# One linear step of an exponential moved from VectorE to GpSimd, with a ring buffer and two more exp tiles

## The chip, the cores and the metric

The kernel runs on one core of a Trainium2 chip. The metric is the device time of one execution in microseconds (us), the median of several runs. In some of them the record shows a TensorE clock below full speed for some time: a mean of 0.986 instead of 0.998 goes with about 10 us more in the kernel before (942 us instead of 932).

Engines are named as the profile names them: PE is TensorE (PEld its weight loads), ACT is ScalarE, DVE is VectorE, POOL is GpSimd.

## The reference, cut to what matters

The program is one conformer block on x of shape (2, 4000, 144), four heads of 36, in bfloat16. Only the attention concerns us:

```python
h = _layernorm(x, axis=-1)
qkv = h @ w_qkv
# ... split into q, k, v, four heads each ...
scores = jnp.einsum('bhqd,bhkd->bhqk', q, k) * scale
p = _softmax(scores, axis=-1)
att = jnp.einsum('bhqk,bhkd->bhqd', p, v)
```

A feed-forward layer stands before it; a convolution module, a second feed-forward layer and a last normalisation stand behind it.

## The kernel before

The kernel is a Python program that draws up its own schedule. `Rec.op` records an instruction, gives it a start by a small cost model (when its engine is free, when its inputs are ready), and keeps that order. A list scheduler picks what to record next; its choices hang on tables of numbers (`POLICY`), one value for each of 49 stretches of the run. When all is recorded, each engine gets its instructions in the recorded order, with semaphore waits between engines. An engine whose next instruction is late stands still; e8_sel50 below shows such a stop of 4.18 us.

Queries are worked in 16 chunks of 500; each chunk has 63 score tiles (62 full ones of 128 x 1000, a small one at the end). PE makes the scores in PSUM. The exponential is then made in one of two ways. ACT does it in one instruction. For 137 of the tiles DVE does it in a chain: it writes the exponent as an integer (two casts out of PSUM), splits the fraction off (AND), forms a parabola of it (linear step, square), adds that back and halves. The halved 16-bit integer is the bit pattern of a bfloat16.

```python
op("dve", "tensor_scalar", mm, zz, 0xFF, 0x6400, op0=ALU.bitwise_and, op1=ALU.bitwise_or, ...)   # AND
yield need("dve")
off, sc = (E2[1] - 1) / (2 * E2[2]), (256 * E2[2]) ** 0.5
op("dve", "tensor_scalar", mf, mf, sc / 256, (off - 4) * sc, op0=ALU.mult, op1=ALU.add, ...)     # linear step
yield need("dve")
op("dve", "tensor_tensor", mf, mf, mf, op=ALU.mult, ...)                                         # square
yield need("dve")
op("dve", "tensor_tensor", zz, zz, mf, op=ALU.add, ...)                                          # add
# ... give back tile y ...
op("dve", "tensor_scalar", zz, zz, 256 * (E2[0] - 1) - (off * sc) ** 2, 0.5, op0=ALU.add, op1=ALU.mult, ...)  # halve
```

`zz` and `mm`/`mf` are two views into exp tiles (`PT`, nine of them). PE then multiplies the tile with the values. GpSimd normalises rows for the layers around the attention (`XN<-X,RS` in the profile).

The softmax here doesn't subtract the row's maximum and nothing guards it: scores larger than these inputs give would overflow.

## Time and profile before

| | before |
|---|---|
| time, median (lowest to highest) | 932.76 us (931.62 to 932.99, 3 runs) |
| ACT, DVE, POOL busy | 895.0, 849.9, 306.1 us of 929.6 |
| exp tiles of 1000 columns on ACT / on DVE | 855 / 137 |

The lines of the profile that carry the reading stand in the prediction below. The chain of waits that ended last, by engine:

```profile
ACT 47%; PE 36%; DVE 14%; issue 1%; POOL 1%; DMA 0%; POOLq 0%; DVEq 0%
```

ACT and PE hand work to each other for 83% of the span.

### The profile page before, as it was taken

The numbers are of one execution on the slowest core, as the hardware profiler recorded it, in microseconds if no ns is written. First come the engines' busy times: TensorE is split into PE (matmuls) and PEld (weight loads), VectorE is DVE, ScalarE is ACT, GpSimd is POOL, SyncE is SP. The second block draws the span as 40 slices with busy tenths as digits, with TensorE's granted clock in tenths as the row PEclk, the third lists the DMA queues.
The fourth block names the chain that finished last, engine by engine and source line by source line (L and its number), as shares of the span: only waits on it lengthen the run. The fifth ranks groups of instructions, "written<-read, shape, count | busy, mean of one in ns | idle before, by whom it ended". The sixth has DMA issues, their size and how long they took to land.

```text
span 929.6 us, 26576 instructions
## 1 busy us (share of the span) xinstructions
PE 886.9 (95%) x11413; PEld 405.4 (44%) x11413; DVE 849.9 (91%) x1880; ACT 895.0 (96%) x1142; POOL 306.1 (33%) x520
## 2 busy tenths in 40 slices
PE   8999999999999999999999999999999999999997
PEld 7444433434344344344443443443444343434456
DVE  8886799999989999998999999898999999997997
ACT  6899999999999999999999999999999999999985
POOL 4220140182115412351512452225415331441433
PEclk9999999999999999999999999999999999999999
DMA  4000000000000000000000000000000000000000
GB/s 124 22 2 1 2 2 1 1 2 1 2 2 2 2 2 2 2 2 1 9 1 1 14 2 8 2 1 14 2 8 3 7 2 9 8 1 8 8 2 26
DMA packets 7449, 7.30 MB, mean 8 GB/s; under 512 B 2381, under 2 KB 7332, under 8 KB 7332
## 3 DMA queue, kind: packets, MB, share of 16 engines
q1 hardware_dynamic: 5918, 5.00, 1.8%
q8 instruction: 89, 1.46, 0.6%
q10 hardware_dynamic: 1414, 0.62, 0.3%
q14 instruction: 28, 0.23, 0.1%
HBM read 3.31 MB, written 2.30 MB: 6 GB/s over the span
## 4 chain that ended last, share of the span: by engine, by line
ACT 47%; PE 36%; DVE 14%; issue 1%; POOL 1%; DMA 0%; POOLq 0%; DVEq 0%
ACT PT L169 41%; PE PS L169 36%; DVE PT L169 8%; ACT TH L169 5%; DVE ST L169 2%; DVE HT L169 1%; DVE X L169 1%; DVE QT L169 1%; DVE OTF L169 1%; POOL RS L169 0%; DMA X<-in_x_dram 0%; DVE DG L169 0%; POOL XN L169 0%; DVE XN L169 0%; DVE XT L169 0%
## 5 line engine op out<-in xcount | busy, mean ns | idle before, releaser
L169 ACT ACTIVATE PT<-PS 128x1000 bf16<-128x1000 f32 (+1 forms) x871 | 802.4, 1053 | 6.8 <-PE PS L169 5.2
L169 PE MATMUL PS<-QT,KT 64*64 64x500 bf16 x3968 | 413.9, 385 | 20.3 <-ACT PT L169 14.2
L169 PE MATMUL PS<-PT,VA 64*37 64x500 bf16 x3968 | 353.4, 374 | 4.9 <-DVE OTF L169 2.2
L169 PEld LDWEIGHTS PS<-QT,KT 64*64 64x64 bf16 x3968 | 122.4, 104 | 219.7 <-ACT PT L169 139.1
L169 POOL TENSOR_SCALAR RS<-ST 125x4 f32<-125x4 f32 x112 | 41.6, 371 | 467.2 <-DVE ST L169 462.5
L169 DVE TENSOR_SCALAR PT<-PS 128x500 uint16<-128x500 f32 x274 | 183.0, 669 | 12.8 <-PE PS L169 11.5
L169 DVE TENSOR_TENSOR PT<-PT 128x1000 uint16<-128x1000 uint16 (+1 forms) x274 | 184.0, 676 | 1.5
L169 DVE TENSOR_SCALAR PT<-PT 128x1000 uint16<-128x1000 uint16 (+1 forms) x411 | 163.8, 415 | 2.3
L169 PEld LDWEIGHTS PS<-PT,VA 64*37 64x37 bf16 x3968 | 114.1, 95 | 111.1 <-issue 31.9
L169 POOL TENSOR_SCALAR XN<-X,RS 125x144 bf16<-125x144 bf16 x224 | 149.9, 680 | 5.8
L169 POOL TENSOR_TENSOR RS<-RS,NHALF 125x4 f32<-125x4 f32 (+1 forms) x103 | 100.5, 980 | 112.5 <-DVE RS L169 107.8
L169 ACT ACTIVATE TH<-PS 128x500 bf16<-128x500 f32 (+2 forms) x198 | 104.3, 549 | 5.0 <-PE PS L169 4.3
L169 DVE SCALAR_TENSOR_TENSOR HT<-TH,PS 128x500 bf16<-128x500 bf16 (+1 forms) x135 | 80.8, 614 | 9.6 <-ACT TH L169 9.4
L169 PE MATMUL PS<-XT,WA 72*128 72x500 bf16 (+2 forms) x288 | 73.8, 355 | 2.9 <-DVE HT L169 1.6
L169 DVE SCALAR_TENSOR_TENSOR X<-PS,X 125x288 bf16<-125x288 f32 x128 | 57.0, 451 | 15.3 <-PE PS L169 13.6
L169 DVE BATCH_NORM_STATS2 ST<-X 125x6 f32<-125x288 bf16 x160 | 65.5, 446 | 1.2 <-DMA X<-in_x_dram 1.0
L169 PE MATMUL PS<-WB,HT 128*125 128x144 bf16 (+1 forms) x640 | 52.8, 230 | 0.5 <-DVE HT L169 0.5
L169 PEld LDWEIGHTS PS<-WB,HT 128*125 128x125 bf16 (+1 forms) x640 | 44.1, 136 | 14.0 <-issue 4.2
L169 PE MATMUL PS<-IDENT,XN 125*72 125x125 bf16 x512 | 42.2, 221 | 2.5 <-DVE HT L169 1.3
L169 DVE COPY XT<-PS 72x1000 bf16<-72x1000 bf16 (+1 forms) x66 | 39.9, 609 | 3.1 <-PE PS L169 2.6
L169 PEld LDWEIGHTS PS<-IDENT,XN 125*72 125x72 bf16 x512 | 31.5, 112 | 21.0 <-issue 10.6
L169 PE MATMUL PS<-U,DG 128*128 128x250 bf16 (+5 forms) x204 | 34.3, 265 | 0.6 <-DVE PT L169 0.4
(88 smaller groups left out, 579.6 us busy)
## 6 DMA issues: line engine op xcount, KB each, us to landing
X<-in_x_dram SPq DMA_DIRECT2D x16, 140.6 KB
out_dram<-XN SPq DMA_DIRECT2D x13, 140.6 KB
out_dram<-XN SPq DMA_DIRECT2D x4, 70.3 KB
WA<-in_w_ff1a_dram ACTq DMA_DIRECT2D x1, 144.0 KB
WB<-in_w_ff1b_dram ACTq DMA_DIRECT2D x1, 144.0 KB, 2.6
WA<-in_w_ff2a_dram SPq DMA_DIRECT2D x1, 144.0 KB
WB<-in_w_ff2b_dram SPq DMA_DIRECT2D x1, 144.0 KB
WQKV<-in_w_qkv_dram ACTq DMA_DIRECT2D x1, 121.5 KB
```

The lines of the kernel that those rows point to most:

```text
L169: ins = getattr(eng, o.name)(*o.a, **o.k)
```

## The change

The intent: DVE is nearly full while GpSimd is idle two thirds of the time. If GpSimd does the linear step, DVE has room for more tiles, and ACT, the fullest engine, has fewer to do. The trip over GpSimd keeps exp tiles longer, so two are added; their memory comes from `XTQ`, which held the normed rows of a whole batch (4000 columns) and becomes a ring of four chunks. All schedule tables are new.

```diff
-    NPT = 9
+    NPT = 11
+    XR, XD = 4, 16
     ... (every POLICY table has new values) ...
+    GPOOL = 1
+    GSLACK = 1.5
+    GCOST = 1.6
-    XTQ = sb("XTQ", [2, T])
+    XTQ = sb("XTQ", [2, XD + XR * CH])
     ... (projections read XTQ at c % XR; the last 16 columns are copied for tiles across the seam) ...
     def pre2(c):
-        yield need("dve")
+        yield need("dve", cond=lambda: c < XR or (c - XR in q_done and c - XR + 1 in v_done))
     ...
-        yield need("dve")
+        pool = GPOOL and R.free["pool"] < R.free["dve"] + GSLACK
+        yield need("pool" if pool else "dve")
-        op("dve", "tensor_scalar", mf, mf, sc / 256, (off - 4) * sc, op0=ALU.mult, op1=ALU.add, r=[("M", y, 0)],
-           w=[("M", y, 1)], cost=c_dve(2 * CH, 4))
+        op("pool" if pool else "dve", "tensor_scalar", mf, mf, sc / 256, (off - 4) * sc, op0=ALU.mult, op1=ALU.add,
+           r=[("M", y, 0)], w=[("M", y, 1)], cost=GCOST if pool else c_dve(2 * CH, 4))
```

## The prediction

> **What bounds the kernel now.** I read the busy table first, then the windows by stage, then the groups of instructions, then short stretches of the timeline. The page's first table (engine, busy us, share of the span, instructions):
>
> ```profile
> PE 886.9 (95%) x11413; PEld 405.4 (44%) x11413; DVE 849.9 (91%) x1880; ACT 895.0 (96%) x1142; POOL 306.1 (33%) x520
> ```
>
> Three engines stand over 90%, so the table alone does not name the bound. The Trainium skill, "Perfetto Trace Analysis", section "Identifying the Most-Contended Engine", says to judge VectorE, ScalarE and GpSimd by occupancy, and that matmul occupancy is a poor measure of how close TensorE is to its limit; weight-load occupancy is better. Here weight loads are 44%, so I set PE's 95% aside and look at the others by stage (columns: window, length, then PE, PEld, DVE, ACT, POOL busy us with counts, clock, DMA share, GB/s):
>
> ```profile
> 0.00:50.00 50.00, 45.31 (x540) 30.03 (x541) 42.41 (x137) 36.63 (x63) 17.53 (x37) 1.00 0.24 68
> 50.00:150.00 100.00, 97.02 (x1254) 40.20 (x1254) 78.89 (x195) 97.75 (x121) 19.41 (x33) 1.00 0.01 2
> 150.00:200.00 50.00, 47.88 (x646) 21.19 (x642) 48.69 (x102) 49.47 (x60) 17.71 (x28) 1.00 0.01 2
> 200.00:900.00 700.00, 673.81 (x8697) 293.86 (x8694) 657.25 (x1367) 693.92 (x861) 240.82 (x407) 1.00 0.02 4
> 900.00:930.00 30.00, 22.89 (x291) 20.13 (x288) 22.63 (x82) 17.22 (x41) 10.60 (x15) 0.97 0.07 21
> ```
>
> From 200 to 900 us ACT is busy 693.92 of 700 (99%) and DVE 657.25 (94%). ACT is the bound of the long middle, with DVE close behind; GpSimd stands at 34% there. Only the first 50 and the last 30 us leave ACT idle (13 us each), and the change does not address those. The groups that matter (name, count | busy, mean ns | idle before):
>
> ```profile
> L169 ACT ACTIVATE PT<-PS 128x1000 bf16<-128x1000 f32 x855 | 794.4, 1061 | 5.6 <-PE PS L169 4.0
> L169 DVE TENSOR_SCALAR PT<-PS 128x500 uint16<-128x500 f32 x274 | 183.0, 669 | 12.8 <-PE PS L169 11.5
> L169 DVE TENSOR_SCALAR PT<-PT 128x1000 uint16<-128x1000 uint16 x274 | 110.0, 415 | 1.5
> L169 DVE TENSOR_TENSOR PT<-PT 128x1000 uint16<-128x1000 uint16 x137 | 92.4, 677 | 0.6
> L169 DVE TENSOR_TENSOR PT<-PT 128x1000 f16<-128x1000 f16 x137 | 92.3, 676 | 0.9
> L169 DVE TENSOR_SCALAR PT<-PT 128x1000 f16<-128x1000 f16 x137 | 56.9, 415 | 0.8
> L169 POOL TENSOR_SCALAR XN<-X,RS 125x144 bf16<-125x144 bf16 x224 | 149.9, 680 | 5.8
> ```
>
> The softmax's exponential is made in two ways: 855 full tiles by one ScalarE instruction, 137 tiles by a seven-instruction VectorE chain. The split is the balance between the two engines: each tile that VectorE takes over is one less on ACT. The change frees VectorE, so it pays only as far as more tiles go over (or VectorE's lateness was holding ACT, which the 1% idle in the middle says it hardly was).
>
> Recorded lengths overlap by the write's tail, so I take starts. ACT: seven exp tiles in a row occupy 699.77 to 705.95, 0.88 us each. DVE: start to start, an AND 0.33, a PSUM cast 0.59, the linear step 0.32; two tensor-by-tensor steps took 1.38 together at 405.59, the next at 406.89, 0.65 each.
>
> ```profile
> 699.77 6.42 ACT L169 ACTIVATE PT<-PS 128x1000 bf16<-128x1000 f32 x7
> 705.95 0.51 ACT L169 ACTIVATE TH<-PS 128x250 bf16<-128x250 f32 x1
> ...
> 226.07 0.41 DVE L169 TENSOR_SCALAR PT<-PT 128x1000 uint16<-128x1000 uint16 x1
> 226.40 0.67 DVE L169 CAST QT<-PS 128x500 bf16<-128x500 f32 x1
> 226.99 0.41 DVE L169 TENSOR_SCALAR PT<-PT 128x1000 f16<-128x1000 f16 x1
> 227.31 0.67 DVE L169 CAST QT<-PS 128x500 bf16<-128x500 f32 x1
> ```
>
> So a VectorE tile costs that engine 2 x 0.59 + 2 x 0.65 + 3 x 0.33 = 3.5 us now, and 3.1 us without the linear step.
>
> **What the Trainium skill says.** "SBUF — State Buffer", section "SBUF: two separate sides": VectorE and GpSimd share one pair of SBUF ports as an exclusive lock; a VectorE instruction in a two-port mode, or with two SBUF inputs, and a GpSimd instruction block each other, whichever starts first. Four of the chain's steps are of that kind: the AND, the two tensor-by-tensor steps, the last add. The trace agrees with blocking, but not evenly. Durations, min/median/max:
>
> ```profile
> L169 POOL TENSOR_SCALAR XN<-X,RS x224: 453/462/3222, 127.4 to 895.4; 125x144 bf16<-125x144 bf16 x112
> L169 DVE TENSOR_SCALAR PT<-PT x411: 365/409/603, 91.8 to 894.3; 128x1000 uint16<-128x1000 uint16 x97, 128x1000 f16<-128x1000 f16 x40
> L169 DVE TENSOR_TENSOR PT<-PT x274: 626/668/825, 94.0 to 893.3; 128x1000 f16<-128x1000 f16 x124, 128x1000 uint16<-128x1000 uint16 x13
> ```
>
> A GpSimd row can be pushed from 0.46 to 3.22 us; a VectorE step loses at most 0.2 us. Laying the starts side by side, VectorE is delayed when it starts some 180 to 310 ns after a GpSimd row's start, and then until about 315 ns after it: a 144-element row holds the ports some 150 ns, about 1.05 ns an element, though its record lasts 460. A GpSimd row thus yields to VectorE before it has begun and blocks it while it streams. At 1000 elements the hold would be some 1.05 us, seven times longer, and no VectorE step in this trace has met that. "GPSIMD Engine Reference", section "Elementwise — side-by-side cycle accounting", gives 1.03 cycles an element for simple bodies; the 1.05 ns is near it.
>
> **The change, part by part.**
> (a) Removed from VectorE: up to one 0.33 us step per tile, 137 x 0.33 = 45 us at most. The builder moves it only if it thinks GpSimd free within 1.5 us of VectorE. GpSimd's normalisation bursts (two small steps, a power of about 1.04 us, four rows) occupy a third of the middle, so I choose 85%: 116 steps, 38 us.
> (b) Added to GpSimd: some 0.2 fixed + 1.05 streaming = 1.25 us alone (estimate from the rows above), about 1.6 with the waits that rows show here (mean 680 against 462). 116 x 1.6 = 186 us, so GpSimd goes to about 490 us, 53%. Not a bound, but rows and steps queue behind one another.
> (c) Port stalls put back on VectorE. I put a hold of 1.05 us at each of the 137 linear steps of this trace, let it wait for a VectorE step under way, and counted the following port-using steps, except the square that needs its result: 41 are hit, 15 us in all, 0.11 us each. With a 1.4 us hold it is 0.25 us. I take 0.11 x 116 = 13 us.
> (d) Net VectorE time freed: 38 - 13 = 25 us. Spending x more tiles there costs 3.1x and shortens the run by 0.88x, which at 91% use takes 0.8x of VectorE's room: 25 = 3.9x, x = 6 to 7, **6 us off ACT's path**.
> (e) Buffers: nine to eleven exp tiles. A VectorE tile holds two through its chain, and the GpSimd hop lengthens it by over 1 us; the two extra tiles mostly pay for that.
> (f) The ring for normed rows: projections of chunk c wait for chunk c-4's queries and values. In the first batch this pulls queries of chunks 2 and 3 forward, three to five casts of 0.59 us each into a stretch where VectorE has room (79% from 50 to 150 us). About zero. A copy of 16 columns every fourth chunk is nothing.
> (g) The retuned schedule tables: nothing in the profile prices them. ACT's idle in the middle is 6 us, so they can win 2 or 3 us there and as much at the ends. I allow 3 us.
> Sum: 932.8 - 6 - 3 = about **924 us**.
>
> **The rivals.** *The port lock gives it all back*: if the step holds the ports 1.4 us or more, stalls reach 0.25 us and over, and the square waits for a late GpSimd. Then VectorE frees nothing, the planned extra tiles make it late, ACT starves: 930 to 938. For it: a 3.22 us row; the builder's cost model has no lock. Against: VectorE lost at most 0.2 us so far. *All gain, no stall*: 45 us freed, x = 45/3.9 = 11.5, 10 us off, with retuning about 918; against it stands the lock. *GpSimd becomes a bound*: normalised rows come late and projections starve; at 53% I do not believe it. *A transfer matters*: DMA share is 0.02; no.
>
> **Range and chances.** Between full gain with good retuning (915) and everything given back (933). Over 2% faster needs under 914.5, which is beyond the no-stall sum; 0.10. Over 2% slower needs over 951; 0.03.
>
> **What will show it.** A group of GpSimd steps writing exp tiles, about 116, mean near 1.6 us; more than 137 PSUM-read pairs on VectorE (about 144) and fewer than 855 ACT tiles (about 848); the maxima of AND and tensor-by-tensor steps rising from 603 and 825 ns to 1.4 us or more; ACT still 99% busy in the middle. I am wrong if VectorE takes over 12 tiles or more, if the tile count is unchanged but the time falls (then buffers or retuning did it), or if the square's wait for GpSimd shows among the longest waits.

## The result, and the profile after

| | before | after |
|---|---|---|
| time, median (lowest to highest) | 932.88 us (931.62 to 933.14, 4 runs) | 944.66 us (944.53 to 944.97, 4 runs) |
| ratio, 95% interval | | 1.0129 (1.0112 to 1.0147) |
| exp tiles of 1000 columns on ACT / on DVE | 855 / 137 | 850 / 142 |

The changed kernel is 1.3% slower, outside the range of the prediction.

The changed kernel's busy table, and two of its windows (same columns as in the prediction):

```profile
PE 889.9 (94%) x11420; PEld 402.5 (43%) x11420; DVE 851.0 (90%) x1802; ACT 895.2 (95%) x1138; POOL 436.8 (46%) x633
```

```profile
200.00:900.00 700.00, 665.18 (x8550) 286.58 (x8547) 653.00 (x1291) 681.13 (x841) 356.63 (x506) 1.00 0.02 4
900.00:945.00 45.00, 34.44 (x418) 25.06 (x416) 31.99 (x95) 29.13 (x56) 14.82 (x24) 0.95 0.05 14
```

ACT's busy total is the same as before to 0.3 us. Between 200 and 900 us it is busy 681.13 us where it was busy 693.92: 12.8 us more idle. The loss builds up there: the work missed in the middle is done after 900. (Busy time is not a pure measure of work: e1_pow below has the same ACT instructions and reads 890.0 us busy, 5.2 less. Five tiles fewer on ACT, some 4.4 us by the prediction's 0.88 us each, therefore don't show in this total.) DVE is no fuller than before, so the bound did not move to it. The chain of the changed kernel:

```profile
PE 34%; DVE 30%; ACT 30%; POOL 4%; issue 1%; DMA 0%; POOLq 0%; DVEq 0%
```

DVE's share of the chain went from 14% to 30%. Its groups in the changed kernel (count | busy, mean ns | idle before), to be set against the same groups in the prediction:

```profile
L169 DVE TENSOR_SCALAR PT<-PT 128x1000 uint16<-128x1000 uint16 x284 | 125.2, 453 | 1.2
L169 DVE TENSOR_TENSOR PT<-PT 128x1000 uint16<-128x1000 uint16 x142 | 103.0, 728 | 0.6
L169 DVE TENSOR_TENSOR PT<-PT 128x1000 f16<-128x1000 f16 x142 | 97.6, 689 | 2.2 <-POOL PT L169 2.1
```

The AND and halving steps grew from 415 to 453 ns, the adds from 677 to 728, the squares from 676 to 689. The square's wait for GpSimd is only 2.1 us in the whole run, so the trip as such is hidden. The durations as min/median/max tell how the means grew:

```profile
L169 DVE TENSOR_SCALAR PT<-PT x319: 364/411/1128, 101.4 to 906.2; 128x1000 uint16<-128x1000 uint16 x140, 128x1000 f16<-128x1000 f16 x20
L169 DVE TENSOR_TENSOR PT<-PT x284: 627/669/1498, 104.2 to 905.3; 128x1000 f16<-128x1000 f16 x126, 128x1000 uint16<-128x1000 uint16 x16
```

The medians stayed, the maxima nearly doubled: a minority of steps is held up. The moved step on GpSimd:

```profile
L169 POOL TENSOR_SCALAR PT<-PT x107: 1024/1029/2310, 101.9 to 901.6; 128x1000 f16<-128x1000 f16 x107
```

One such hit in the changed kernel's timeline, DVE first (start us, length us), then GpSimd:

```profile
815.12 0.45 DVE L169 TENSOR_TENSOR AN<-PS,RD 125x288 bf16<-125x288 f32 x1
815.49 1.35 DVE L169 TENSOR_TENSOR PT<-PT 128x1000 uint16<-128x1000 uint16 x1
816.76 0.41 DVE L169 TENSOR_SCALAR PT<-PT 128x1000 uint16<-128x1000 uint16 x1
```

```profile
815.29 1.02 POOL L169 TENSOR_SCALAR PT<-PT 128x1000 f16<-128x1000 f16 x1 [1.25 <-DVE PT L169]
```

The add starts 0.20 us after the GpSimd step and takes 1.35 us instead of 0.67: if its usual length is taken off the end, it stands still until 0.88 us after that step's start, and only then runs. Laid side by side, the hits on a GpSimd step that was not itself delayed all end their standstill 0.88 to 0.89 us after its start. A DVE step that is already under way goes first, and the GpSimd step is the longer one. One that begins just after the GpSimd step is mostly shut out: of the three chain steps that began in its first 0.17 us, those at 0.11 and 0.15 us were held up by 0.77 and 0.83 us, and only the third went first. So the step shuts DVE out until 0.88 us after its start. (The expectations below, and the planner of e11_aware, reckon with a hold of 0.72 us that begins 0.165 us after the start. These traces don't bear out that free beginning.)

How that reaches ACT shows on PE (the group of the matmuls with the values, before and after; idle before, what ended it):

```profile
L169 PE MATMUL PS<-PT,VA 64*37 64x500 bf16 x3968 | 353.4, 374 | 4.9 <-DVE OTF L169 2.2 <-ACT PT L169 1.0 <-DVE PT L169 0.8
L169 PE MATMUL PS<-PT,VA 64*37 64x500 bf16 x3968 | 357.5, 375 | 9.3 <-DVE PT L169 6.1
```

Before, these matmuls waited 0.8 us for DVE's tiles; now 6.1. In PE's recorded order the next scores stand behind them, so they come late and ACT waits for them. ACT's waits for PE ahead of exponentials, before and after (us in total, times, longest):

```profile
ACT PT L169 <- PE PS L169: 5.2, 16, 0.5
ACT PT L169 <- PE PS L169: 14.6, 32, 1.3
```

### The profile page after: what moved, and what is told of

It reads as the page before. It is cut to its first block, busy times and chain, and to the rows that moved or that the text cites. A ratio compares the mean times of both kernels' runs of the same rounds, so it can differ in the third digit from the quotient of the medians.

```text
span 942.8 us, 26578 instructions
## 1 busy us (share of the span) xinstructions
PE 889.9 (94%) x11420; PEld 402.5 (43%) x11420; DVE 851.0 (90%) x1802; ACT 895.2 (95%) x1138; POOL 436.8 (46%) x633
## 4 chain that ended last, share of the span: by engine, by line
PE 34%; DVE 30%; ACT 30%; POOL 4%; issue 1%; DMA 0%; POOLq 0%; DVEq 0%
PE PS L169 34%; ACT PT L169 26%; DVE PT L169 19%; ACT TH L169 4%; DVE ST L169 2%; DVE HT L169 2%; POOL RS L169 2%; DVE X L169 2%; POOL XN L169 2%; DVE XT L169 1%; DVE QT L169 1%; DVE SW L169 1%; DVE AN L169 0%; DMA X<-in_x_dram 0%; DVE U L169 0%
## 5 line engine op out<-in xcount | busy, mean ns | idle before, releaser
L169 PE MATMUL PS<-PT,VA 64*37 64x500 bf16 x3968 | 357.5, 375 | 9.3 <-DVE PT L169 6.1
L169 POOL TENSOR_SCALAR PT<-PT 128x1000 f16<-128x1000 f16 x107 | 123.2, 1151 | 302.6 <-DVE PT L169 301.6
L169 DVE TENSOR_SCALAR PT<-PS 128x500 uint16<-128x500 f32 x284 | 189.3, 669 | 18.5 <-PE PS L169 17.2
L169 DVE TENSOR_TENSOR PT<-PT 128x1000 f16<-128x1000 f16 (+1 forms) x284 | 199.4, 709 | 2.9 <-POOL PT L169 2.1
L169 DVE TENSOR_SCALAR PT<-PT 128x1000 uint16<-128x1000 uint16 (+1 forms) x319 | 139.3, 450 | 1.4
L169 POOL TENSOR_TENSOR RS<-RS,NHALF 125x4 f32<-125x4 f32 (+2 forms) x101 | 97.0, 965 | 81.4 <-DVE RS L169 76.6
L169 DVE SCALAR_TENSOR_TENSOR HT<-TH,PS 128x500 bf16<-128x500 bf16 (+1 forms) x140 | 83.4, 614 | 14.9 <-ACT TH L169 14.5
L169 POOL TENSOR_SCALAR RS<-ST 125x4 f32<-125x4 f32 x114 | 43.9, 385 | 95.4 <-DVE ST L169 89.4
L169 DVE SCALAR_TENSOR_TENSOR X<-PS,X 125x288 bf16<-125x288 f32 (+1 forms) x128 | 57.1, 451 | 10.4 <-PE PS L169 9.0
```

The costliest lines, as they stand in the source:

```text
L169: ins = getattr(eng, o.name)(*o.a, **o.k)
```

## The experiments

**Theory.** The GpSimd step shuts the ports that the DVE chain needs. The order of all engines was drawn up by a cost model that knows no ports. A stall that the order does not know of makes DVE late, then PE, then ACT, and the bound engine's lost time is not won back. **Rivals.** The trip over GpSimd itself (hop); the new tables being worse on the chip; the step simply belonging on DVE.

Building one part of the change without another is no clean test: any edit that alters a recorded cost or choice shifts every later choice. So most experiments keep the recorded order of all engines **exactly** and replace the instruction that is issued at a place. The replay then is:

```diff
-                    ins = getattr(eng, o.name)(*o.a, **o.k)
+                    todo = getattr(o, "pre", []) + [(o.name, o.a, o.k)] + getattr(o, "post", [])
+                    for name, args, kw in todo:
+                        ins = getattr(eng, name)(*args, **kw)
```

**e1_pow: same trip, ports free.** A power of 125 x 4 numbers takes GpSimd as long as the step (mean 1146 against 1151 ns) but reads and writes next to nothing. The result lacks the correction.

```diff
+        if pool:
+            o.name, o.a, o.k = "tensor_tensor", (SCR[0:TB, y, 0, :], PONE[0:TB, :], NHALF[0:TB, :]), dict(op=ALU.pow)
-        op("dve", "tensor_tensor", mf, mf, mf, op=ALU.mult, ...)
+        op("dve", "tensor_tensor", mf, mf, mf, op=ALU.subtract if pool else ALU.mult, ...)
     ... (the halving step gets another constant)
```

> The changed kernel with the order of every engine's instructions untouched; only the 107 linear steps on GpSimd are replaced by a power of 125x4 numbers (1.04 us, the same length as the step's 1.02 to 1.03 us alone) that waits for the AND and is waited for by the square in the same way, but hardly touches SBUF. Wrong on purpose (the square becomes a difference, so the correction is left out). PORT THEORY (the step holds the SBUF ports some 0.72 us, VectorE stalls by about 20 us in sum, and the fixed order turns that into about 16 us of lateness): the time falls by 12 to 16 us, to 929 to 933. HOP RIVAL (the trip over GpSimd, not the ports, makes the square and all behind it late): within 3 us of 944.7. TABLES RIVAL (the new schedule tables are just worse on the chip): within 3 us of 944.7.

Measured: 930.91 us (930.69 to 931.05), 13.8 us less than the changed kernel; the kernel before took 931.71 in the same rounds (ratio 0.999). The DVE groups and the middle window of e1_pow:

```profile
L171 DVE TENSOR_SCALAR PT<-PT 128x1000 uint16<-128x1000 uint16 x284 | 114.4, 415 | 1.2
L171 DVE TENSOR_TENSOR PT<-PT 128x1000 uint16<-128x1000 uint16 x142 | 95.9, 678 | 0.6
L171 DVE TENSOR_TENSOR PT<-PT 128x1000 f16<-128x1000 f16 x142 | 95.6, 675 | 2.1 <-POOL SCR L171 1.9
```

```profile
200.00:900.00 700.00, 672.95 (x8690) 293.58 (x8689) 646.50 (x1317) 686.99 (x856) 361.08 (x514) 1.00 0.02 4
```

The lengths are back at 415, 678 and 675 ns. Against these the changed kernel's stalls sum to 284 x 38 + 142 x 50 + 142 x 14 ns = 19.9 us. Taking them away, with order and trip unchanged, takes 13.8 us off the time, and DVE's share of the chain falls from 30% to 12%: the port theory holds, hop and tables fall as the cause of the loss. One us of stall cost 0.69 us. The run says a second thing: **without any stall from the step, the change is worth 0.8 us at most** (the interval of the ratio, 0.9973 to 1.0007, includes no gain), though DVE was relieved of 107 steps of 0.33 us, 35 us in all. The tiles did come off ACT: over the whole run it is busy 890.0 us against 895.0 in the kernel before. But its idle time grew from 34.6 to 39.3 us, and its waits for PE ahead of the tile `TH` alone from 4.3 to 9.6 us.

**e2_split2, e4_hold2, e5_pow2: the size of hold and trip.** The step as two halves; the step after a second pass into a scratch tile; two powers.

```diff
 # e2_split2: o becomes the first half, the second follows at once
+            parts_ = [(o.name, (mf[:, j:j + 500], mf[:, j:j + 500]) + tuple(o.a[2:]), o.k) for j in range(0, 2 * CH, 500)]
 # e4_hold2
+            o.pre = [(o.name, (SCH[:, nsc[0] % 4, :],) + tuple(o.a[1:]), o.k)]
 # e5_pow2: as e1_pow, and once more
+            o.post = [(o.name, (SCR[0:TB, y, 1, :],) + o.a[1:], o.k)] * 1
```

> Same order; each linear step on GpSimd is two instructions of 500 elements, so each holds the ports half as long. Right results. PORT THEORY: stalls about half as long for about as many hits, 5 to 8 us less, 937 to 940. HOP RIVAL: the step takes about 0.2 us longer in all, so no gain, 945 to 950. TABLES RIVAL: 943 to 947.

> Same order; each GpSimd step is preceded by a second pass of the same size into a scratch tile, so ports are held twice as often and the trip takes about 2 us (the plan reckons with 1.6). Right results. PORT THEORY: stalls about double, plus some waits of the square: 15 to 30 us more, 960 to 975. TABLES RIVAL: under 955.

> As e1_pow, but with two powers one after the other: the trip takes about 2 us as in e4_hold2, the ports stay free. Wrong on purpose. PORT THEORY: within 6 us of e1_pow (929 to 939), far below e4_hold2. HOP RIVAL: close to e4_hold2, 955 or more.

Measured: 943.54, 984.78 and 949.97 us. Only e4's direction came as foretold, and it went past its range; the other two missed. (e2 lies in the range of the tables rival, which e1_pow had already ruled out.) The two doubled trips both make the square wait for GpSimd (waits of DVE in e4_hold2, then in e5_pow2: us in total, times, longest):

```profile
DVE PT L171 <- POOL PT L171: 29.4, 40, 1.5
```

```profile
DVE PT L171 <- POOL SCR L171: 28.0, 45, 1.9
```

At 1.15 us the trip makes the squares wait only 1.9 us in all (e1_pow); with two powers it costs 19 us more. The order had been drawn up with 1.6 us. At nearly equal trips e4 is 34.8 us over e5, and 32.3 us if only runs at full clock are taken (981.6 against 949.3). By the same sum its stalls come to 37.9 us, about twice the changed kernel's: twice the stall cost more than twice e1's 13.8. The split halved the stalls (284 x 22 + 142 x 24 + 142 x 7 ns = 10.6 us) but brought 1.1 us. Two things may have eaten the rest, and no run parts them: the squares' waits for GpSimd rose from 2.1 to 7.1 us, and TensorE's clock was lowered in all four runs of e2 (0.985 to 0.996; the changed kernel had 0.998 to 0.999). In the profiled one it was at half for 6.8 us after a pause of PE of 1.64 us. Whether smaller holds are a remedy stays open.

**e3_ondve: the same order, the steps on DVE.**

```diff
+        if pool:
+            o.lin = True                     # at emission
+            if getattr(o, "lin", False):     # when all is recorded, ahead of the semaphores
+                o.eng = "dve"
```

> The changed kernel, order untouched, with the 107 linear steps put back on VectorE at the places where GpSimd was to do them: VectorE gets 107 x 0.33 = 35 us that the order has no room for, the ports are free of the step. LATENESS THEORY (in a fixed order each us of unplanned VectorE time costs about 0.68 us: e1_pow took 20.2 us of stall away and gained 13.8 us): 930.9 + 0.68 x 35 = 955, 948 to 960. RIVAL (the step belongs on VectorE, the move to GpSimd is the fault by itself): faster than 944.7, near e1_pow, 930 to 940.

Measured: 948.85 us, at the low end: 35 us that the order did not know of cost 17.9 us over e1_pow, 0.5 per us (the trip is gone in e3 as well). The rival falls; the moved step costs more on DVE than on GpSimd in *this* order.

**e7_inject: unplanned DVE time in the kernel before.** Is it ports at all, or any time that the order does not know of?

```diff
+        if n % 2 == 0:
+            o.pre = [(o.name, (SCH[:, :], zz[:, 0:CH]) + tuple(o.a[2:]), o.k)]    # a second AND, 500 elements
```

> The kernel before with its order untouched; 65 of its 137 VectorE tiles get one extra AND of 500 elements into a scratch tile in front of their own AND, about 0.20 us each, 13 us in all that the order does not know of; no GpSimd step, no new port use by GpSimd. LATENESS THEORY at 0.68 a us: 9 us more, 937 to 944. RIVAL (VectorE stood 6% idle in the middle, such time is absorbed): under 935.

Measured: 941.88 us against 932.08. The 65 extra steps take 13.1 us from start to next start and cost 9.8 us, 0.75 per us, in a kernel whose DVE stood 6% idle in the middle. (Two of the four runs had a slightly lowered clock; the two at full clock took 941.3 us, 0.7 per us.) No step was moved to GpSimd, and the chain's lengths stayed (418, 674 and 676 ns). An extra AND is of the kind that shares ports, so a small part may be GpSimd's lateness: its rows took 705 ns in the mean instead of 680. In the main the price is that of lateness in a fixed order; in the changed kernel the ports are what made DVE late.

**e6_nopool: the new tables without the step.**

```diff
-    GPOOL = 1
+    GPOOL = 0
```

> The changed kernel built with the GpSimd step switched off; ring, eleven exp tiles and new tables stay, so the builder draws up another order. TABLES RIVAL (the tables are good, the step spoils them): 925 to 932. THEORY (tables are fitted to one order each and are worth nothing once it shifts): 938 to 950, no better than the changed kernel although no step holds the ports.

Measured: 952.14 us, above even the range given. Nothing holds the ports, and it is slower than both. The edit makes the builder draw up another order, for which the tables were never fitted; it can't tell what the step is worth, and I read no more from it.

**e8_sel50, e9_sel75, e10_sel49: the step moved only where the ports are free.** In the order of the kernel before, with its tables and nine tiles, a linear step goes to GpSimd only if the order has room for the trip, no port-using DVE step begins meanwhile and GpSimd is idle.

```diff
+    for o1, o2, o3, o4 in chain:                 # AND, linear step, square, add
+        t0 = o1.t0
+        if o3.t0 - t0 < 1.45:                    # e9: 1.1
+            continue
+        if any(t0 + 0.45 < p < t0 + 1.35 and p not in (o1.t0, o2.t0, o3.t0) for p in ports):
+            continue
+        if any(p0 < t0 + 1.45 and p1 > t0 + 0.3 for p0, p1 in busy):     # e9: 1.1
+            continue
+        if before_[id(o2)] > t0 + 0.4:           # e10 only
+            continue
     ... (the step's time is added to busy)
+        o2.eng = "pool"
```

> The kernel before with its order untouched (nine exp tiles, old tables, no ring); only those 50 of 137 linear steps go to GpSimd for which the plan shows at least 1.45 us from the AND to the square, no port-using VectorE step starting in between, and GpSimd idle. Right results. LATENESS THEORY: next to no stall is added (under 3 us in sum against 20 in the changed kernel), 50 x 0.33 = 16 us of VectorE time is freed, which can win back part of the 7 us by which the old order runs behind its plan: 926 to 930. RIVAL (any port-holding step on GpSimd costs more than it frees): 933 to 938. RIVAL (freed VectorE time is worth nothing in a fixed order): 931 to 933.

> As e8_sel50 with the shorter limit of 1.10 us from AND to square: 75 steps move, some of which make the square wait for GpSimd by up to 0.5 us. LATENESS THEORY: little more than e8 or a loss, 927 to 933. If trips did not matter: 1 to 2 us below e8.

Measured: 938.74 and 963.28 us, both misses, though the stalls are as small as before. In e8 most of it is one event. GpSimd, then DVE and PE in e8's timeline:

```profile
575.26 1.80 POOL L171 TENSOR_SCALAR XN<-X,RS 125x144 bf16<-125x144 bf16 x4
...
577.15 1.03 POOL L171 TENSOR_SCALAR PT<-PT 128x1000 f16<-128x1000 f16 x1
578.22 0.68 DVE L171 TENSOR_TENSOR PT<-PT 128x1000 f16<-128x1000 f16 x1 [4.18 <-POOL PT L171]
...
579.54 0.60 PE L171 MATMUL PS<-XT,WA 72*128 72x500 bf16 x2 [3.48 <-DVE HT L171]
```

My selection looked at planned times, but GpSimd runs in recorded order, and this step had been recorded behind a normalisation that comes later. DVE waited 4.18 us, PE stood still 3.48 us. The next window shows a second price (TensorE's granted clock is third from the right):

```profile
580.00:582.50 2.50, 2.50 (x19) 0.71 (x22) 2.47 (x7) 1.63 (x3) 0.00 (x0) 0.58 0.00 0
```

The clock fell to half for 3.4 us after PE's pause. The Trainium skill, "TensorE: Matmul & The Clock Gate", section "What's actually happening", says that after an idle window of about 3.4 us the array's clock drops to half; this trace agrees. (Other profiles here show the half clock after shorter pauses; see the last section.) e9 has several such events (mean clock 0.979 to 0.984 in all its runs). Without that step:

> As e8_sel50 without the one step that e8's trace shows stuck on GpSimd behind a later normalisation row (VectorE waited 4.2 us for it at once). If that queue place was e8's whole loss: 931 to 934. If freed VectorE time did win something once it is gone: 926 to 930. If the other 49 trips cost something too: 935 or more.

Measured: 933.18 us against 931.70 (ratio 1.0017, interval 1.0001 to 1.0034). So the queue place and what followed it was most of e8's loss, and moving 49 steps at next to no stall, 16 us of DVE time freed, wins nothing. In a fixed order no tile can go over from ACT, so this run doesn't test what freed time is worth to an order drawn up for it.

**e11_aware, e13_aware_pow: a builder that knows of the ports.** The cost model gets the port rule with the numbers that I had read from the traces (the start of the hold set too late, see above), and the tables were searched again for its own order.

```diff
-    GCOST = 1.6
+    GCOST = 1.03
+    HOLD = 0.72
     # in Rec.op
+        if hold:
+            h0 = start + 0.165
+            for a0, a1 in self.ports[-12:]:
+                if a0 <= h0 < a1 + 0.1:
+                    h0 = a1 + 0.1
+            self.holds.append((h0, h0 + hold))
+            cost += h0 - start - 0.165
+        if port and eng == "dve":
+            for h0, h1 in self.holds[-6:]:
+                if h0 <= start < h1:
+                    start = h1
+            self.ports.append((start, start + cost))
     ... (the chain's DVE steps are recorded with port=True, the GpSimd step with hold=HOLD)
```

> The changed kernel with a builder that knows of the ports: a GpSimd step is reckoned at 1.03 us, waits for the VectorE step under way and then shuts the ports for 0.72 us, and a port-using VectorE step planned into that time is planned after it; tables searched again for this builder's own order. THEORY (the fault was stalls the order did not know of): it runs behind its own order by no more than the kernel before does, 929 to 935, 10 us or more below the changed kernel. RIVAL (sharing the ports is a loss however it is planned): 938 or more.

Measured: 936.26 us, 8.4 less than the changed kernel, 1.3 above the range given; the kernel before took 931.70. Its DVE groups:

```profile
L182 DVE TENSOR_SCALAR PT<-PT 128x1000 uint16<-128x1000 uint16 x274 | 119.8, 449 | 1.7
L182 DVE TENSOR_TENSOR PT<-PT 128x1000 uint16<-128x1000 uint16 x137 | 98.6, 721 | 0.7
L182 DVE TENSOR_TENSOR PT<-PT 128x1000 f16<-128x1000 f16 x137 | 94.1, 687 | 5.1 <-POOL PT L182 4.6
```

The stalls are nearly as large as in the changed kernel: 274 x 34 + 137 x 43 + 137 x 12 ns = 16.8 us, with 112 steps on GpSimd. As the order is another one, this alone does not part stall from ignorance of it. The last run does, with e1's stand-in in e11's order:

> The kernel of e11_aware, order untouched, with the 112 GpSimd steps replaced by the power stand-in of e1_pow (same trip, ports free). Wrong on purpose. e11's stalls sum to 16.8 us, e1_pow's removal of 19.9 us gained 13.8 us. IF PLANNED STALLS ARE HARMLESS: it gains at most 4 us, 932 to 937. IF A STALL COSTS THE SAME PLANNED OR NOT (about 0.7 a us): it gains 10 us or more, 923 to 927, faster than the kernel before.

Measured: 934.07 us (933.66 to 934.39 and one run of 941.95), against 932.35 before; stalls gone (418, 675, 676 ns). That is 2.2 us below e11, or 2.8 if each is set against the kernel before of its own rounds. **The same kind of stall costs 13.8 us for 19.9 us in the order that does not know of it, and 2 to 3 us for 16.8 us in the one that does.** Two limits: the two orders differ in their tables too, and this is one order of each kind; and the sum leaves out what it costs an order to keep room for stalls. Without any stall e13 is still 1.7 us slower than the kernel before.

**e12_ring: buffers and ring without the step, tables searched again.**

> Ring and eleven exp tiles without any GpSimd step, tables searched again for this order. If the buffers alone are worth something once the order is fitted: 926 to 931, faster than both. If not: 932 or more.

Measured: 931.64, 935.43, 941.35 and 941.45 us, inconclusive: in the slower three the clock was reduced, in the profiled one to half for 23.9 us from 39 us on. The one run at a mean clock of 0.997 is level with the kernel before (931.3 to 931.9). It beats the changed kernel, not the old one. No version with right results beats the old kernel.

## Why the prediction was wrong

*What bounds the kernel, and where a loss would show*: right. The difference shows as ACT's idle time in the middle.

*Part (a)*, 116 steps moved: 107 were. *Part (b)*, 1.25 us alone and 1.6 with waits: 1.03 alone, 1.15 with waits.

*Part (c)*, the stalls: I put 13 us on a hold of 1.05 us, seven times a short row's 0.15 us. It did not scale so: the row's lock ended about 0.315 us after its start, that of the 1000-element step at 0.88 us. To find support in "1.03 cycles an element" was a slip as well, as it set cycles against nanoseconds. Some 47 steps were hit (counted as steps over 30 ns too long, 91 against 44 in e1_pow), 19.9 us in all. Mis-sized, but of the right kind.

*Part (d)* is the step that failed, "Net VectorE time freed: 38 - 13 = 25 us". It takes DVE time as a stock: freed and stalled time add up, and the rest turns into tiles at 3.9 us each. What failed first is the price of the stalls: they were not paid out of DVE's room at 0.88/3.9 = 0.23 a us but out of the run, at 0.69 a us (13.8 us for 19.9 us, e1_pow), in an order drawn up without them. The other half failed at its last step. DVE's freed time did turn into tiles, five where I had reckoned six or seven, and ACT was busy 5.0 us less in e1_pow. But the 6 us "off ACT's path" did not arrive: ACT idled 4.7 us more, and 0.8 us at most was left. *Parts (e) and (g)* can't be priced singly: what tables, ring and tiles give together with the step is those 0.8 us; *(f)* was not tested alone.

*The rivals.* "The port lock gives it all back" named the cause, and even that the cost model has no lock; I set it aside because no DVE step had yet lost more than 0.2 us, and because I tied it to a hold of 1.4 us. A lock that ended at 0.88 us was enough. Its 930 to 938 was still too low. GpSimd did not become a bound (46%), as I had said, and the DMA share stayed at 0.02.

*The signs.* Most came: 107 steps on GpSimd, 142 pairs of casts, 850 tiles on ACT, longer maxima (1498 ns, but only 1128 for the ANDs, where I had said 1.4 us), no long wait of the square. The one that failed was "ACT still 99% busy in the middle": it was 97%.

What stays open: why ACT, with five tiles fewer and no stall, idled longer in e1_pow, so that freed DVE time won next to nothing. PE's order and the number of tiles in flight are candidates; no run here parts them.

## What to carry to other kernels

Ask first who paid for the schedule: where each engine runs a fixed order, time that the order does not know of on a *non*-bound engine can go to the end at 0.5 to 0.75 us a us (e1, e3, e7), even when that engine is idle 6% of the time; and time freed there is worth only what the bound engine can use. Moving a GpSimd-sized elementwise step off VectorE is not free when both use the shared SBUF ports: look for a doubled maximum beside an unchanged median, and put the measured hold into the planner before tuning (here that won back 8.4 of some 12 us, not all). To tell a cost from a reshuffled schedule, keep the order and swap the instruction.

## What the Trainium skill lacked or had wrong

- "SBUF — State Buffer", section "SBUF: two separate sides", says that whoever starts first has the port pair for the whole instruction. The exclusive lock is confirmed, but the recorded lengths are not its bounds: a GpSimd step recorded as 1.02 to 1.03 us shut VectorE out until 0.88 us after its start. Beside a 144-element row in the kernel before, chain steps that started up to 0.12 us after the row were held up by 0.06 us at most and the row took 0.69 us or more instead of 0.46; those that started 0.18 to 0.31 us after a row that was not itself delayed waited until about 0.315 us. The page has no such numbers.
- "GPSIMD Engine Reference", section "Elementwise — side-by-side cycle accounting", gives 1.03 cycles an element for simple bodies and says nothing of the hold. The 1000-element multiply-add took 1.03 us in all and shut VectorE out until 0.88 us. The page's figure comes to 0.86 us for 1000 elements at its 1.2 GHz (an estimate from the page), which is near that.
- No page says what port contention costs a kernel with a fixed order: 19.9 us of stall cost 13.8 us unplanned, 16.8 us cost 2 to 3 us planned.
- "TensorE: Matmul & The Clock Gate", section "What's actually happening", ties the half clock to an idle window of about 3.4 us, which e8_sel50 bears out (3.48 us pause, then half for 3.4 us). In four other profiles the half clock came with a shorter pause of PE, during it or within 1.1 us of its end: 1.64 us in e2_split2, 1.96 in e5_pow2, 2.20 in e7_inject, 2.60 in e6_nopool; a pause of 2.56 us in e4_hold2 was not followed by it. Apart from the ends of the runs, its stretches lasted 3.41, 6.83, 13.65 or 23.9 us, whole multiples of 3.41. In e12_ring it lasted 23.9 us with no pause over 0.5 us in the 20 us before (PE busy 89% of them). In its section "A second HAM failure mode: psum-queue depth-cycling" the page also tells of short pauses between groups of matmuls that lower the clock when they come often; no run here shows whether this was such a case.
